# Moving q and k between partition halves with ScalarE and GpSimd in the first batch

## The chip, the cores and the metric

The kernel runs on one core of a Trainium2 chip. A core has a matrix engine (TensorE: PE for the products, PEld for the loads of its weights), VectorE (DVE), ScalarE (ACT) and GpSimd (POOL), each of which works through its own queue of instructions in order, and SyncE (SP), whose queue here issues all DMA transfers; 16 DMA engines carry them out. On-chip memory has 128 partitions. An engine's copy may read from one half of the partitions and write to the other.

The metric is the device time of one execution in microseconds (us).

## The reference

Attention with a cluster mask, followed by a feed-forward network with a maximum over three products:

```python
q_assign = np.argmax(np.einsum('bhsd,hcd->bhsc', q_n, c_n), axis=-1)
k_assign = np.argmax(np.einsum('bhsd,hcd->bhsc', k_n, c_n), axis=-1)
mask = q_assign[:, :, :, None] == k_assign[:, :, None, :]
scores = scale * np.matmul(q, k.transpose(0, 1, 3, 2))
scores = np.where(mask, scores, -1000000000.0)
attn = softmax(scores)            # with 1e-9 added to the sum
x = (attn @ v)                    # [b s, h d]
h = np.maximum(np.maximum(x @ w1, x @ w2), x @ w3)
out = h @ w_out
```

There are 4 batches, 8 heads, 768 positions, 64 dimensions a head and 16 clusters; the network has width 512 and 768 hidden columns. The inputs are float32, the weights float64.

## The kernel before

Products of float32 numbers are made of parts. Each of q and k is split into hi and lo, so that a score is a sum of products of parts. Two heads (a *pair*) are prepared together. The input has q of a head in partitions 0 to 63 and k in partitions 64 to 127, so the preparation of a pair begins with both in the same columns and must bring parts of k to the lower half and parts of q to the upper half. The tile `qk` of a pair has four blocks of two heads by 768 columns, named `AQ, BQ, BK, AK`; in the end they hold [q lo; q hi], [q hi; onehot], [k hi; onehot of k] and [k hi; k lo].

For a pair, in order:

- `qk_prep` (L357), once for each head: SP loads the head (L352), ScalarE copies its hi part into BQ (L362), and VectorE or GpSimd (nearly always GpSimd) subtracts to put the lo part into AQ (L365).
- `cluster_scores` (L397): PE multiplies both parts by the centroids.
- `qk_moves` (L367): three transfers between places on the chip. L370 takes k hi from the upper half of BQ and writes it to the lower halves of BK and AK, 768 KB by the profile's account. L371 copies k lo within the upper half from AQ to AK, 384 KB. L372 takes q hi from the lower half of BQ to the upper half of AQ, 384 KB; since it writes what L371 reads, it waits for L371.
- `cluster_rows` (L415): VectorE and GpSimd find the cluster of each position (L420 to L438). Four small transfers (L448) write the onehot rows into BQ and BK. All pairs use one buffer, `cl_t`, which is free again once these transfers have landed.

The first pair of all has its own moves, by ScalarE (`first_k_moves`) and GpSimd (`first_q_moves`). Two pairs keep their onehot rows in DRAM and load them again later (L390).

The attention goes in steps, `scores` (L470): one step is 128 queries of a head against its 768 keys. PE makes the scores (L475, L477; the second needs the onehot rows), VectorE scales and finds the maximum (L480), ScalarE takes the exponential (L483), then ScalarE and VectorE split the probabilities into two float16 parts (L493, L494), or for some steps GpSimd and ScalarE (L489 to L491). SP issues a transposing transfer (L495), and two steps after the head's last one PE multiplies by v (L505, L508). The first batch goes through its heads twice, with half of the queries each time; pair 0 is loaded and prepared a second time for that. So `qk_moves` is called four times in the first batch: for pairs 1, 2, 3 and again for pair 0. After that it is called for each pair of the three later batches.

During the first batch the float64 weights are loaded (L192), made into float32 by ScalarE and VectorE (L194, L196), and split (L205 to L207). The feed-forward network (L540 to L591) of one half or batch runs beside the attention of the next; that of the last batch stands alone at the end.

The order of each engine's instructions is planned when the program is built. The kernel gives every piece of work a priority, mostly the number of its step plus an offset (the pair after the first has `P1_LATE = -10`, so ten steps early), and a planner with a model of the times (`schedule_with_timeline_sim=True`, L759) picks, for each engine, what is ready and has the best priority. On the chip the order is fixed, and semaphores hold back what isn't ready.

Of the kernel before, what the change touches and what calls it, by code (L numbers as in the profile page):

```python
# [8 lines left out]
F32 = mybir.dt.float32  # L9
# [14 lines left out]
def kernel(  # L24
# [11 lines left out]
    """Cluster-masked softmax attention followed by a three-way maxout FFN.  # L36

    Float32 products are split exactly. Scores and cluster scores use float32r parts
    (x = hi + lo, 12 significant bits each); the probabilities, values and the FFN use
    float16 parts of operands scaled by powers of two that come from the largest  # L40
    magnitude of the operand, found on the chip.

    The argmax over the clusters is the same for q and for q / (|q| + 1e-6), a positive
    factor per row, so only the centroids are normalised. The mask is a product of one-hot
    rows inside the score product: it adds 0 where the clusters agree and -2^100 where
    they don't, which absorbs the score.
    """
# [48 lines left out]
    def pow2_scale(cols, name):  # L96
        """p: the power of two at or below the largest magnitude; s = 2^14 / p; on all partitions."""
        m = sb.tile([P, 1], F32, tag="sc_m", name="sc_m", bufs=2)
        nc.vector.tensor_reduce(m, cols, axis=AX.X, op=ALU.max)
        nc.vector.tensor_scalar_max(m, m, 1e-30)  # L100
        nc.vector.tensor_scalar(m.bitcast(I32), m.bitcast(I32), 0x7F800000, None, op0=ALU.bitwise_and)
        a = one()[:, 0:P]
        nc.tensor.matmul(a, m.bitcast(BF16)[:, 1:2].broadcast_to([P, P]), ident16, start=True, stop=True)
        p = cpool.tile([P, 1], F32, name=f"p_{name}")
        s = cpool.tile([P, 1], F32, name=f"s_{name}")
        nc.vector.tensor_reduce(p, a, axis=AX.X, op=ALU.max)
        nc.vector.reciprocal(s, p)
        nc.vector.tensor_scalar_mul(s, s, 2.0**14)
        return p, s

    # A load that would run too far ahead is held back to the last step of the attention that
    # has been issued: one element of its tile is first written from the sums of that step.
# [56 lines left out]
    # The weights come as float64; the chip makes float32 of their bits, cut after 23 of the  # L169
    # fraction. The doubles land one halfword off, so that the upper three halfwords are  # L170
    # [fraction 16..31 | fraction 0..15] in one aligned word, and [sign, exponent, four bits]
    # in one that reads as bfloat16. Its upper 8 exponent bits of 11, as float16, have the bias
    # that float32 has for all 11: the float16 bits are the upper 13 bits of the result.
    # Each block of 128 hidden columns has its own power of two; the rows of w_out that
    # meet it carry the ratio to the largest.
# [10 lines left out]
    def convert(wp, src, a, d):  # L186
        """src: int16 quarters of float64 in DRAM [P, a, 4m]; d: float32 [P, a * m] on chip."""
# [155 lines left out]
    # Rows of the input: q of a head over k of it. Per pair of heads:  # L343
    # [q lo; q hi], [q hi; onehot], [k hi; (onehot - 1) 2^100], [k hi; k lo].
# [21 lines left out]

    def qk_moves(b, pr):  # L367
        t = qkt[b, pr].bitcast(F32)
        up, dn = slice(0, D), slice(D, 2 * D)
        nc.sync.dma_start(out=t[up, BK : AK + 1], in_=t[dn, BQ : BQ + 1].broadcast_to([D, 2, 2, S]))  # L370
        nc.sync.dma_start(out=t[dn, AK], in_=t[dn, AQ])  # L371
        nc.sync.dma_start(out=t[dn, AQ], in_=t[up, BQ])  # L372

    # The first pair of all doesn't wait for transfers between partitions.
# [93 lines left out]
    # The probabilities are divided by the sums of their rows as they are split (largest 2^14).  # L468
    # Vector has the most to do: Pool splits some of the tiles.
# [128 lines left out]
    # The first batch goes through its heads twice, one half of the queries at a time, so that  # L598
    # the FFN can start on the first half; q and k of three of its pairs stay on chip.
    V_0, W_0 = 4, 9  # L600
    # Vector's part where a task can go to either: 1; Pool's: 0. The last two pairs of QK_LO are
    # the first of the second batch and the first pair when it is loaded again.
# [33 lines left out]
    def spread(units, first, last, late=0):  # L636
        """Put the units at even distances between two steps; the scheduler sees them later by `late`."""
        for i, u in enumerate(units):
            k = first + i * (last - first) / len(units)
            plan.setdefault(max(int(k // 1), 0), []).append((k + late, u))  # L640
# [122 lines left out]
```

## Time and profile before

| | |
|---|---|
| time, median of 3 runs | 869.12 us (867.17 to 874.3) |
| span of the profiled execution, first to last instruction | 866.7 us |
| PE, PEld busy | 719.4 us (83%), 422.7 us (49%) |
| VectorE, ScalarE, GpSimd busy | 611.4 us (71%), 518.0 us (60%), 494.4 us (57%) |
| DMA | 149.86 MB, mean 173 GB/s |

The page gives no time of the profiled execution other than its span; the lowest of the three runs is 0.5 us above it, the median 2.4.

In a row of a timeline stand the start in us, the duration in us, engine, line, operation, the tiles written and read, their shapes, how many instructions are merged, and in brackets the idle time of the engine before it with what ended that. A row such as `SPq L370` is the issue of a transfer, not the transfer; "DMA to landing" counts from the start of the issue to the arrival. In the row of a line stand the shortest, middle and longest duration in ns. A row of the waits gives the total in us, how often, and the longest.

### The profile page before, as it was taken

The page shows a single profiled execution, that of the slowest core. Times are in us where ns is not written, and L with a number is a line of the kernel's source. Part 1 is how long each engine was busy: PE and PEld are TensorE (multiplying, and loading weights), DVE is VectorE, ACT ScalarE, POOL GpSimd, SP SyncE. Part 2 cuts the span into 40 slices and gives each one's busy share as a digit, 9 for nine tenths or more (in the row PEclk, how much of TensorE's full clock was granted, in tenths as well). Part 3 has the DMA queues.
Part 4 walks back from the last instruction along what each step waited for, and adds up shares of the span by engine and source line. Part 5 has one row for each costly group of instructions (what it writes and reads, how often), then busy time and mean ns, then how long its engine had stood idle before and what let it go on. Part 6 is the DMA issues. An engine that isn't in the chain of part 4 may idle for free.

```text
span 866.7 us, 12102 instructions
## 1 busy us (share of the span) xinstructions
PE 719.4 (83%) x3836; PEld 422.7 (49%) x3836; DVE 611.4 (71%) x1327; ACT 518.0 (60%) x907; POOL 494.4 (57%) x486
## 2 busy tenths in 40 slices
PE   3445576767688998989898989989898999999997
PEld 2322343344354565545565545545555565556463
DVE  6777988798989898977798766876587667411020
ACT  6555668754867587868585756765767577510101
POOL 5687783583957374765786555785575446412111
PEclk9656576887889999999999999999999999999999
DMA  8999878999999999999999999897898676810100
GB/s 263 244 200 207 190 156 166 219 227 185 242 184 217 231 196 204 215 176 221 227 198 202 223 211 170 168 228 164 171 175 156 148 148 110 158 43 1 37 1 36
DMA packets 331263, 149.86 MB, mean 173 GB/s; under 512 B 304704, under 2 KB 313920, under 8 KB 331200
## 3 DMA queue, kind: packets, MB, share of 16 engines
q1 hardware_dynamic: 331200, 149.10, 83.2%
q8 instruction: 30, 0.49, 0.2%
q14 instruction: 33, 0.27, 0.1%
HBM read 38.57 MB, written 7.08 MB: 53 GB/s over the span
## 4 chain that ended last, share of the span: by engine, by line
PE 27%; DMA 19%; DVE 14%; ACT 9%; issue 7%; POOL 5%; SPq 2%; ACTq 0%; POOLq 0%; DVEq 0%
DMA pt<-hl 17%; PE one L546 13%; PE one L580 7%; DVE hl L494 5%; DVE big L480 4%; ACT e L483 3%; ACT hl L493 3%; PE one L505 2%; DMA stage<-in_v_dram 2%; POOL hl L491 2%; PE one L508 1%; PE big L475 1%; DVE onehot L434 1%; PE big L477 1%; SPq L495 1%
## 5 line engine op out<-in xcount | busy, mean ns | idle before, releaser
L494 DVE SCALAR_TENSOR_TENSOR hl<-e,r,hl 128x768 f16<-128x768 f32 x147 | 194.3, 1326 | 48.0 <-ACT hl L493 45.2
L546 PE MATMUL one<-x,w16a 128*128 128x384 f16 x1152 | 205.9, 332 | 18.2 <-DVE vf_h L558 9.8
L483 ACT ACTIVATE e<-big,nm 128x768 f32<-128x768 f32 x192 | 172.1, 897 | 77.4 <-DVE big L480 31.4
L480 DVE TENSOR_SCALAR_CACHE_REDUCE big<-big 128x768 f32<-128x768 f32 x192 | 181.8, 959 | 12.7 <-PE big L477 12.2
L493 ACT ACTIVATE hl<-e,r 128x768 f16<-128x768 f32 x147 | 135.9, 931 | 72.7 <-DMA pt<-hl 62.4
L475 PE MATMUL big<-qk 128*128 128x512 f32 (+1 forms) x384 | 128.0, 417 | 61.4 <-ACT e L483 59.6
L546 PEld LDWEIGHTS <-w16a 128*128 128x128 f16 x1152 | 110.2, 99 | 100.8 <-issue 36.1
L477 PE MATMUL big<-qk 80*128 80x512 f32 (+1 forms) x384 | 111.6, 374 | 15.5 <-DMA qk<-cl_t 12.7
L475 PEld LDWEIGHTS big<-qk 128*128 128x128 f32 x384 | 68.2, 209 | 96.0 <-ACT e L483 77.1
L546 PE MATMUL one<-x,w16b 128*128 128x384 f16 x576 | 101.8, 331 | 6.1 <-ACT xt L514 2.6
L505 PE MATMUL one<-pt,v 128*128 128x384 f16 x384 | 84.6, 358 | 17.3 <-DMA pt<-hl 9.1
L491 POOL TENSOR_TENSOR hl<-e,hl 128x768 f16<-128x768 f32 x45 | 77.6, 1730 | 27.6 <-ACT hl L490 27.1
L477 PEld LDWEIGHTS big<-qk 80*128 80x128 f32 x384 | 67.2, 212 | 28.2 <-issue 11.2
L546 PEld LDWEIGHTS <-w16b 128*128 128x128 f16 x576 | 55.1, 99 | 46.7 <-issue 13.7
L365 POOL TENSOR_TENSOR qk<-stage,qk 128x768 fp32r<-128x768 f32 x32 | 64.2, 2021 | 17.9 <-ACT qk L362 17.8
L518 POOL TENSOR_TENSOR xs<-xs,xt 128x384 f32<-128x384 f32 x32 | 34.7, 1084 | 61.9 <-ACT xt L514 61.9
L558 DVE SCALAR_TENSOR_TENSOR vf_h<-one,vf_h 128x384 f32<-128x384 f32 x48 | 26.4, 550 | 51.5 <-PE one L546 51.5
L505 PEld LDWEIGHTS <-v 128*128 128x128 f16 x384 | 37.1, 106 | 50.9 <-issue 24.9
L564 POOL TENSOR_SCALAR wf_h<-wf_h 128x384 f16<-128x384 f32 x24 | 15.5, 647 | 77.0 <-DVE wf_h L558 73.1
L489 POOL TENSOR_SCALAR e<-e,r 128x768 f32<-128x768 f32 x45 | 46.5, 1035 | 21.1 <-DVE r L485 9.6
L558 DVE SCALAR_TENSOR_TENSOR wf_h<-one,wf_h 128x384 f32<-128x384 f32 x48 | 26.5, 551 | 45.4 <-PE one L546 45.2
L490 ACT CAST hl<-e 128x768 f16<-128x768 f32 x45 | 37.2, 830 | 33.6 <-DMA pt<-hl 20.0
(130 smaller groups left out, 1042.8 us busy)
## 6 DMA issues: line engine op xcount, KB each, us to landing
stage<-in_qk_dram SPq DMA_DIRECT2D x36, 384.0 KB, 4.6
qk<-qk SPq DMA_DIRECT2D x16, 768.0 KB, 7.0
qk<-qk SPq DMA_DIRECT2D x32, 384.0 KB, 5.0
stage<-in_v_dram SPq DMA_DIRECT2D x25, 384.0 KB, 4.8
wd<-in_moe_w_dram SPq DMA_DIRECT2D x18, 512.0 KB, 4.6
out_dram<-o SPq DMA_DIRECT2D x24, 256.0 KB, 2.4
pt<-hl SPq DMA_TRANSPOSE x192, 4.3
wd<-in_moe_w_out_dram SPq DMA_DIRECT2D x6, 512.0 KB, 5.9
```

Of the source, the lines that this page charges most:

```text
L365: last["lo"] = eng.tensor_tensor(t[:, AQ, i], x, t[:, BQ, i].bitcast(F32), op=ALU.subtract)
L475: nc.tensor.matmul(t[:, lo:hi], aq[:, qs], ak[:, lo:hi], start=True, stop=False)
L477: last["pe"] = nc.tensor.matmul(t[:, lo:hi], bq[0:K2, qs], bk[0:K2, lo:hi], start=False, stop=True)
L480: last["nm"] = nc.vector.tensor_scalar(e, e, -SCALE, 3.0e38, op0=ALU.mult, op1=ALU.min, accum_out=nm)
L483: nc.scalar.activation(x, e, AF.Exp, bias=nm, scale=-1.0, accum_out=r)
L491: nc.gpsimd.tensor_tensor(hl[:, 1, :], x, hl[:, 0, :], op=ALU.subtract)
L493: nc.scalar.activation(hl[:, 0, :], x, AF.Copy, scale=r)
L494: nc.vector.scalar_tensor_tensor(hl[:, 1, :], x, r, hl[:, 0, :], op0=ALU.mult, op1=ALU.subtract)
L505: nc.tensor.matmul(t[:, 0:NB], vt, pt[:, :, kt, :], start=(kt == 0), stop=False)
L546: nc.tensor.matmul(t[:, 0:NB], w16[jt // JA][:, jt % JA, wa, i, ct], x16[b, gi, ct][:, xa, :], start=(n == 0), stop=(n == 3 * CT - 1),)
L558: nc.vector.scalar_tensor_tensor(m, t[:, 0:NB], 2.0**-24, ms[jt], op0=ALU.mult, op1=ALU.max)
L580: nc.tensor.matmul(t[:, 0:DM], h16[jt][:, ha, tt * P : (tt + 1) * P], wo16[0][:, jt, wa, :], start=(n == 0), stop=(n == 3 * JT - 1),)
```

## The change

In the first batch alone, the move of k hi and the move of q hi are made by engines. The transfer of k lo (L371) stays. In the later batches nothing changes.

```diff
     def qk_moves(b, pr):
-        t = qkt[b, pr].bitcast(F32)
+        t = qkt[b, pr]
+        x = t.bitcast(F32)
         up, dn = slice(0, D), slice(D, 2 * D)
-        nc.sync.dma_start(out=t[up, BK : AK + 1], in_=t[dn, BQ : BQ + 1].broadcast_to([D, 2, 2, S]))
-        nc.sync.dma_start(out=t[dn, AK], in_=t[dn, AQ])
-        nc.sync.dma_start(out=t[dn, AQ], in_=t[up, BQ])
+        if b:
+            nc.sync.dma_start(out=x[up, BK : AK + 1], in_=x[dn, BQ : BQ + 1].broadcast_to([D, 2, 2, S]))
+        else:
+            nc.scalar.copy(t[up, AK], x[dn, BQ])
+            nc.scalar.copy(t[up, BK], x[dn, BQ])
+        nc.sync.dma_start(out=x[dn, AK], in_=x[dn, AQ])
+        if b:
+            nc.sync.dma_start(out=x[dn, AQ], in_=x[up, BQ])
+        else:
+            nc.gpsimd.tensor_scalar(t[dn, AQ], x[up, BQ], 1.0, 1.0, op0=ALU.mult, op1=ALU.mult)
```

Each of the two ScalarE copies and the GpSimd copy writes 64 partitions by 1536 columns. Beside this the diff only takes out comments, with the numbers of the lines kept up to the changed function.

## The prediction

> **What bounds the kernel now.** I read the page first, for the span and the engines, then the busy time by stretches, because an average over the span mixes stages.
>
> ```profile
> span 866.7 us, 12102 instructions
> ...
> wd<-in_moe_w_dram SPq DMA_DIRECT2D x18, 512.0 KB, 4.6
> ...
> qk<-cl_t SPq DMA_DIRECT2D x56, 48.0 KB, 2.2
> ```
>
> ```profile
> 0.00:50.00 50.00, 20.25 (x54) 13.26 (x54) 39.03 (x74) 30.23 (x51) 32.15 (x48) 0.80 0.94 248
> 50.00:100.00 50.00, 31.57 (x104) 17.87 (x104) 39.03 (x83) 28.21 (x50) 37.71 (x38) 0.59 0.94 202
> 400.00:600.00 200.00, 180.12 (x1034) 108.48 (x1033) 153.51 (x340) 138.38 (x246) 133.53 (x118) 0.99 0.98 200
> ```
>
> The columns of the last three are stretch, length, busy time of PE, PEld, DVE, ACT and POOL, granted clock, DMA share and GB/s. Between 400 and 600 us PE is busy for 90% of the time: it is the bound there. In the first 100 us it is not: PE works 20.25 and 31.57 us of 50, VectorE 39 of 50, while the DMA engines are at 0.94. The three early calls of the changed function lie there, and the fourth at 157 us. So I asked whether somebody waits for a DMA in those places, and then followed the chain of waits and the timelines of single engines around them.
>
> ```profile
> 38.28 0.77 ACT L194 CAST top<-wd 128x512 f16<-128x512 bf16 x1 [5.47 <-DMA wd<-in_moe_w_dram]
> 39.08 0.69 DVE L196 SCALAR_TENSOR_TENSOR wf<-wd,top 128x512 int32<-128x512 int32 x1 [3.86 <-ACT top L194]
> L192 SPq DMA_DIRECT2D wd<-in_moe_w_dram x2: 541/1197/1853, 28.7 to 31.5; - x2
> DMA to landing us min/median/max: 9.6/10.2/10.8
> 49.61 2.92 SPq L448 DMA_DIRECT2D qk<-cl_t  x4
> DMA to landing us min/median/max: 4.6/5.0/5.7
> 56.36 1.62 PE L477 MATMUL big<-qk 80*128 80x512 f32 x4 [5.07 <-DMA qk<-cl_t]
> ```
>
> The first landing line is that of the two weight loads above it, the second that of the four L448 rows. This is one chain. ScalarE stands at the head of its queue for a weight load that took 9.6 us, twice the kernel's median of 4.6. VectorE idles 3.86 us behind it, with the onehot rows of pair 1 (heads 2 and 3) queued behind that; the rows go out at 49.61, need about 5 us where 2.2 is usual, and PE starts pair 1 at 56.36. It is a queue of transfers, and the moves of q and k are in it:
>
> ```profile
> 17.01 0.74 SPq L370 DMA_DIRECT2D qk<-qk  x1
> 21.31 1.80 SPq L370 DMA_DIRECT2D qk<-qk  x1
> 27.61 0.97 SPq L372 DMA_DIRECT2D qk<-qk  x1
> 41.05 0.51 SPq L372 DMA_DIRECT2D qk<-qk  x1
> 42.30 1.82 SPq L370 DMA_DIRECT2D qk<-qk  x1
> 157.77 0.70 SPq L370 DMA_DIRECT2D qk<-qk  x1
> 158.57 17.53 DMA pt<-hl x2
> SPq L372 <- DMA qk<-qk: 5.4, 2, 3.6
> 176.12 0.93 ACT L493 ACTIVATE hl<-e,r 128x768 f16<-128x768 f32 x1 [5.33 <-DMA pt<-hl]
> ```
>
> The 17.53 us are a piece of the chain that ended last: two transposes, issued right behind the 768 KB move at 157.77, and ScalarE waits 5.33 us for them.
>
> **The change, part by part.** *Removed*, four times (pairs 1, 2, 3, and pair 0 when it is loaded again): a 768 KB and a 384 KB transfer, 4.72 MB. At the first stretch's rate (248 GB/s at 0.94 busy, 264 GB/s when full) that is 3.0 + 1.5 = 4.5 us of the DMA engines a pair, 17.9 us in all. This is the most that the transfers can give; the least is nothing. I take what a wait shows:
> - Ahead of the weight load of 28.7 us stand two large moves and one small, 7.5 us; the first has landed by then, but it counts where the queue behind it has not run empty. Even without it, 4.5 us, most of ScalarE's 5.47 goes. The 7.5 is more than ScalarE's 5.47, so VectorE's 3.86 us go whole: -3.9.
> - Ahead of the rows of 49.61 stand the small move of 41.05 and the large one of 42.30, 4.5 us. The rows could come nearer to 2.2 by 2.8 us; the transposes ahead of them stay, so I take -2.0 (0 to -2.8).
> - At 157.77 the transposes lose 3.0 us of queue: -3.0, 0 to -5.3. SP's wait at L372, 3.6 us, also goes from SP; next late there is the load of v, which stands behind the same move and comes earlier with it.
>
> Together -8.9. SP's issue times (0.5 to 1.8 us each) go as well; I count them at nothing, since SP stood behind the same queue.
>
> *Added*, on ScalarE: two copies of 64x1536 a pair.
>
> ```profile
> L379 ACT CAST qk<-stage x2: 831/831/831, 6.8 to 9.3; 64x768 fp32r<-64x768 f32 x2
> 16.15 2.75 ACT L362 CAST qk<-stage 128x768 fp32r<-128x768 f32 x3 [1.58 <-DMA stage<-in_qk_dram]
> 22.75 0.90 ACT L483 ACTIVATE e<-big,nm 128x768 f32<-128x768 f32 x1 [3.85 <-DVE big L480]
> 25.49 0.77 ACT L194 CAST top<-wd 128x512 f16<-128x512 bf16 x1 [1.75 <-DVE wf L196]
> ```
>
> Twice 0.83 is 1.66 us a copy, 3.3 us a pair, 13.3 in all. They need only the casts of L362, on the same engine, and space that nobody reads, so ScalarE doesn't wait for another engine. Pairs 1 and 2 are cast by 18.90; 6.6 us of copies meet idle stretches of 3.85 and 1.75: 1.0 over. For pair 3 I take the same share, 0.5. The fourth stands ahead of the idle 5.33 us above, of which the relief of 3.0 leaves 2.3: 1.0 over. Together +2.5, and 13.3 if all that cover is gone.
>
> *Added*, on GpSimd: one copy a pair, with a new wait. It overwrites q's low rows, which the remaining transfer (L371) must have read. SP used to wait for this; now GpSimd does, and all of its queue waits behind.
>
> ```profile
> L386 POOL TENSOR_SCALAR qk<-qk x2: 827/827/827, 9.7 to 11.8; 64x768 fp32r<-64x768 f32 x2
> 27.31 1.49 POOL L426 TENSOR_TENSOR cl_t<-cl_t 128x384 f32<-128x384 f32 x1 [2.40 <-DVE r L484]
> 174.81 0.91 POOL L334 TENSOR_SCALAR stage<-stage,s_v 128x768 f32<-128x768 f32 x1 [4.09 <-DMA stage<-in_v_dram]
> ```
>
> A copy of 64x1536 is 1.65 us, 6.6 in all. For pair 1 GpSimd has 2.40 us free before the onehot sum at 27.31; for the fourth, 4.09 before 174.81. I take +0.7 for a wait that overruns the first gap. The bound upwards is a rival below.
>
> GpSimd also slows VectorE when both run:
>
> ```profile
> L494 DVE SCALAR_TENSOR_TENSOR hl<-e,r,hl x51: 976/1136/5728, 30.7 to 299.7; 128x768 f16<-128x768 f32 x51
> L494 DVE SCALAR_TENSOR_TENSOR hl<-e,r,hl 128x768 f16<-128x768 f32 x51 | 73.8, 1455 | 4.3 <-ACT hl L493 3.8
> 16.35 0.56 DVE L434 TENSOR_TENSOR onehot<-rank,cl_m 128x384 f32<-128x384 f32 x1
> 188.91 7.39 DVE L434 TENSOR_TENSOR onehot<-rank,cl_m 128x384 f32<-128x384 f32 x1
> ```
>
> In 300 us the 51 splits of L494 took on average 1455 - 976 ns over their shortest, 24.4 us together. GpSimd is busy for 32.15 + 37.71 of the first 100 us, so for about 200 of 300: 0.12 us for one. 6.6 us more of GpSimd add 0.8. The other end is a VectorE that stands still for all of it, 6.6. I take 0.8: it comes from 51 instructions, the 7.39 from one.
>
> The Trainium skill, SBUF — State Buffer, "Who interferes with whom", has a rule here: VectorE instructions with two SBUF inputs and GpSimd instructions that read SBUF share a port pair as an exclusive lock, and the later one blocks fully. The trace agrees: the same instruction takes 0.56 us or 7.39. What the sum would be by the rule stands with the rivals.
>
> Sum: -8.9 + 2.5 + 0.7 + 0.8 = -4.9. The profiled execution's 866.7 become 861.8. The median of the runs, 869.12, lies 2.4 above that span: **864.2 us**. All later work is ordered behind the first batch, and PE bounds most of it, so I let the shift through to the end whole.
>
> **The rivals.**
> *The queue itself sets the pace.* For: the share of 0.94 in both early stretches. Then all 17.9 us show: -17.9 + 4.0 = -13.9, 855.2. Against: VectorE is at 78%, and much of the relief lies where it is busy.
>
> *GpSimd stalls (slower).* L371 stays in SP's queue, behind transposes, and lands late:
>
> ```profile
> L371 SPq DMA_DIRECT2D qk<-qk x1: 1556/1556/1556, 29.3 to 29.3; - x1
> DMA to landing us min/median/max: 10.8/10.8/10.8
> L371 SPq DMA_DIRECT2D qk<-qk x1: 537/537/537, 52.6 to 52.6; - x1
> DMA to landing us min/median/max: 5.4/5.4/5.4
> 41.53 3.59 POOL L365 TENSOR_TENSOR qk<-stage,qk 128x768 fp32r<-128x768 f32 x2 [2.71 <-ACT qk L362]
> ```
>
> These are pairs 2 and 3. If the order puts pair 2's copy ahead of L426 at 27.31, GpSimd waits until 40.1 less the 7.5 us of relief, 32.6: 5.3 + 1.7 = 7.0 late, and the rows of pair 1 with it. If pair 3's stands right behind L365, which ends at 45.1, it waits until 58.0 less 3.0: 9.9 + 1.7 = 11.6. Both are 18.6, less the forecast's 4.9: +13.7, 882.8. Pair 3's alone gives 875.8. It decides from the point where a copy stands ahead of softmax or onehot work in GpSimd's queue. For: the order comes from a cost model that need not know this queue. Against: that model also delays the copy by the transfer that it expects.
>
> *The lock takes it.* By that mechanism at its full price, VectorE stands still for 6.6 us instead of 0.8: +0.9, 870.0. It is the skill's rule named above; the mean of L494 speaks against it.
>
> *The relief is hidden.* If VectorE's order, and no landing, sets the time of the rows, nothing is gained and 4.0 paid: 873.1.
>
> **How the numbers follow.** Chances: forecast 0.44 (its own range 857 to 870: the relief at 157.77 may be 5.3, ScalarE's copies may be covered or not, and the planned order may change elsewhere), queue 0.22, stalls 0.17, lock 0.07, hidden 0.10. One per cent, about what a measurement of this kernel can tell from no change, is 860.4 to 877.8. Faster: the queue case and a little over a third of the forecast's, 0.38. Slower: most of the stalls, and a few of the hidden and the lock's, 0.18. Within: 0.44. The range from 850 to 877 leaves out the far half of the stalls and the ends of the others.
>
> **What would show it.** Right: no ScalarE wait of 5 us for wd near 38 us; the rows of pair 1 out by about 46 and pair 1 on PE by about 50.5; ScalarE's wait at 176 down to about 2; VectorE's L494 mean in 300 us near 1.47. Wrong: a GpSimd wait for qk<-qk of over 5 us with L426, L489 or L491 right behind it, an L434 or L494 of many microseconds beside a GpSimd copy, or a start of pair 1 that doesn't move.

## The result and the profile after

The changed kernel takes **879.87 us** (median of 5, 876.03 to 884.62), the kernel before 869.12. The ratio is 1.0107, with a 95% interval from 1.0076 to 1.0138: about 1% slower. (The quotient of the two medians is 1.012, inside that interval.) The forecast was 864.2 us, and its range ended at 877.

In the changed file every line behind the edited function stands 9 lower: L480 has become L489, L494 L503, L448 L457. The GpSimd copy is L381, the ScalarE copies are L375 and L376, the transfer of k lo is L377. The profile is that of the slowest of the five executions (884.62 us), so the spans of the two profiles differ by 16.1 us where the medians differ by 10.75. First the page of the changed kernel, and its busy time by stretches (stretch, length, PE, PEld, DVE, ACT, POOL, granted clock, DMA share, GB/s; a share counts a packet whole in the stretch in which it starts, so it can pass 1):

```profile
span 882.8 us, 12105 instructions
...
q1 hardware_dynamic: 330304, 144.38, 79.1%
```

```profile
0.00:50.00 50.00, 18.96 (x53) 12.33 (x53) 42.78 (x84) 37.75 (x55) 32.34 (x48) 0.83 0.81 234
50.00:100.00 50.00, 25.71 (x87) 15.47 (x87) 37.05 (x60) 23.53 (x43) 38.21 (x39) 0.59 0.60 124
250.00:300.00 50.00, 36.87 (x179) 21.30 (x178) 47.17 (x118) 31.53 (x55) 22.79 (x23) 0.83 0.84 176
300.00:350.00 50.00, 43.74 (x232) 25.55 (x231) 31.32 (x69) 29.89 (x52) 24.48 (x23) 0.90 0.90 182
```

The same for the kernel before, where the prediction doesn't show it:

```profile
250.00:300.00 50.00, 41.97 (x221) 24.01 (x220) 47.34 (x110) 33.94 (x59) 25.08 (x24) 0.93 1.04 219
300.00:350.00 50.00, 46.00 (x273) 28.32 (x272) 44.60 (x97) 35.81 (x63) 33.19 (x32) 1.00 1.04 206
```

The transfers are gone (149.10 MB in that queue before, 144.38 now), and the DMA share of the first 100 us falls from 0.94 to 0.81 and 0.60. Yet PE does less in the same time (25.71 us instead of 31.57 between 50 and 100), and in the last two stretches, whose code the change doesn't touch, it does less again.

To see where the time goes I number the steps of the attention by their score reductions (L480 before, L489 after), from 0; each starts once in the profile. The first batch ends near step 48, the second near 96.

| start of step, us | 6 | 36 | 39 | 60 | 78 | 96 | 138 | 186 |
|---|---|---|---|---|---|---|---|---|
| before | 57.6 | 159.0 | 181.3 | 285.4 | 343.9 | 400.4 | 550.7 | 724.2 |
| after | 66.9 | 162.8 | 177.0 | 283.3 | 358.0 | 409.5 | 566.7 | 740.4 |
| after less before | +9.3 | +3.8 | -4.4 | -2.2 | +14.1 | +9.1 | +16.0 | +16.2 |

So the profiles show two losses, neither of which begins at a moved operation: 9 us before step 6, won back by step 39, and 18 us from step 60 to step 138. A single difference of a few us is not to be trusted: two of the runs below (e5, e9) have every queue in the order of the changed kernel until past step 60, and their step 60 starts at 277.4 and 281.2 us, not at 283.3. Timelines of the changed kernel at both places, in order of time:

```profile
50.34 3.25 SPq L457 DMA_DIRECT2D qk<-cl_t  x4
56.79 1.62 PE L486 MATMUL big<-qk 80*128 80x512 f32 x4 [0.97 <-DMA qk<-cl_t]
57.80 8.62 DVE L503 SCALAR_TENSOR_TENSOR hl<-e,r,hl 128x768 f16<-128x768 f32 x1
57.95 1.78 POOL L339 TENSOR_TENSOR v<-vf,v 128x384 f16<-128x384 f32 x2
59.70 1.62 POOL L500 TENSOR_TENSOR hl<-e,hl 128x768 f16<-128x768 f32 x1
61.29 0.99 POOL L435 TENSOR_TENSOR cl_t<-cl_t 128x384 f32<-128x384 f32 x1
62.25 3.36 POOL L207 TENSOR_TENSOR w16a<-wf,w16a 128x512 f16<-128x512 f32 x3
66.95 0.95 DVE L489 TENSOR_SCALAR_CACHE_REDUCE big<-big 128x768 f32<-128x768 f32 x1
69.04 0.79 PE L412 MATMUL big<-qk,cw 128*128 128x512 f32 x1 [9.35 <-ACT e L492]
71.55 0.41 PE L413 MATMUL big<-qk,cw 128*128 128x256 f32 x1
72.12 1.47 POOL L381 TENSOR_SCALAR qk<-qk 64x1536 fp32r<-64x1536 f32 x1 [6.52 <-DVE r L494]
176.69 0.92 ACT L338 CAST v<-stage 128x384 f16<-128x384 f32 x2 [1.47 <-POOL stage L334]
305.76 2.67 SPq L457 DMA_DIRECT2D qk<-cl_t  x4
310.63 4.53 SPq L292 DMA_DIRECT2D stage<-in_v_dram  x2
313.84 0.95 DVE L293 TENSOR_REDUCE vmax<-stage 128x1 f32<-128x768 f32 x1 [1.22 <-DMA stage<-in_v_dram]
315.73 5.30 SPq L504 DMA_TRANSPOSE pt<-hl  x2
318.46 0.95 DVE L293 TENSOR_REDUCE vmax<-stage 128x1 f32<-128x768 f32 x1 [3.41 <-DMA stage<-in_v_dram]
319.33 0.96 DVE L489 TENSOR_SCALAR_CACHE_REDUCE big<-big 128x768 f32<-128x768 f32 x1
```

Near 58 us VectorE stands in L503 for 8.62 us beside GpSimd instructions without a gap, and steps 6 to 8 stand behind it. The delay then reaches the change's own copy for pair 3 (72.12), ahead of which GpSimd idles 6.52 us with softmax work queued behind. The row names VectorE's `r`, which the copy doesn't read. But the copy overwrites rows that the centroid products (L413) read, and it starts 0.16 us after the last of them has ended (71.96); these products are late because PE stands 9.35 us for an exponential (69.04), and ScalarE makes that from the scores held up behind L503.

Near 313 us VectorE's queue holds two maxima of v (L293) ahead of step 67. Each needs a load into a staging buffer, and the second load goes out only when the first maximum has freed its buffer, behind which the transposes of 315.73 stand in SP's queue too. In the kernel before, the same place reads:

```profile
304.06 5.17 SPq L495 DMA_TRANSPOSE pt<-hl  x3
309.32 2.72 SPq L448 DMA_DIRECT2D qk<-cl_t  x4
311.54 0.95 DVE L480 TENSOR_SCALAR_CACHE_REDUCE big<-big 128x768 f32<-128x768 f32 x1
316.19 0.93 DVE L293 TENSOR_REDUCE vmax<-stage 128x1 f32<-128x768 f32 x1
322.86 0.94 DVE L293 TENSOR_REDUCE vmax<-stage 128x1 f32<-128x768 f32 x1
```

Step 67 (311.54) stands ahead of both maxima, and three transposes ahead of the rows. Nothing in the diff asks for that difference: the planner has made a new order of every queue, from start to end, because a few operations of the first batch differ.

### The profile page after: what moved, and what is told of

It reads as the page before. It is cut to its first block, busy times and chain, and to the rows that moved or that the text cites. A ratio compares the mean times of both kernels' runs of the same rounds, so it can differ in the third digit from the quotient of the medians.

```text
span 882.8 us, 12105 instructions
## 1 busy us (share of the span) xinstructions
PE 722.7 (82%) x3836; PEld 425.1 (48%) x3836; DVE 617.5 (70%) x1327; ACT 529.3 (60%) x915; POOL 498.3 (56%) x490
## 3 DMA queue, kind: packets, MB, share of 16 engines
q1 hardware_dynamic: 330304, 144.38, 79.1%
## 4 chain that ended last, share of the span: by engine, by line
PE 26%; DMA 15%; DVE 13%; ACT 7%; issue 6%; POOL 4%; SPq 2%; ACTq 0%; POOLq 0%; DVEq 0%
PE one L555 13%; DMA pt<-hl 12%; PE one L589 6%; DVE big L489 4%; DVE hl L503 4%; ACT hl L502 3%; DMA stage<-in_v_dram 2%; PE one L514 2%; ACT e L492 2%; SPq L504 1%; POOL hl L500 1%; PE big L484 1%; PE one L517 1%; PE big L486 1%; DVE cl_t L441 1%
## 5 line engine op out<-in xcount | busy, mean ns | idle before, releaser
L503 DVE SCALAR_TENSOR_TENSOR hl<-e,r,hl 128x768 f16<-128x768 f32 x147 | 194.9, 1331 | 56.7 <-ACT hl L502 54.6
L489 DVE TENSOR_SCALAR_CACHE_REDUCE big<-big 128x768 f32<-128x768 f32 x192 | 181.6, 960 | 16.2 <-PE big L486 15.7
L514 PE MATMUL one<-pt,v 128*128 128x384 f16 x384 | 82.5, 356 | 38.0 <-DMA pt<-hl 15.3
L500 POOL TENSOR_TENSOR hl<-e,hl 128x768 f16<-128x768 f32 x45 | 78.9, 1759 | 45.4 <-ACT hl L499 44.9
L498 POOL TENSOR_SCALAR e<-e,r 128x768 f32<-128x768 f32 x45 | 43.7, 975 | 28.0 <-DVE r L494 21.0
```

The source lines that it names most:

```text
L489: last["nm"] = nc.vector.tensor_scalar(e, e, -SCALE, 3.0e38, op0=ALU.mult, op1=ALU.min, accum_out=nm)
L500: nc.gpsimd.tensor_tensor(hl[:, 1, :], x, hl[:, 0, :], op=ALU.subtract)
L503: nc.vector.scalar_tensor_tensor(hl[:, 1, :], x, r, hl[:, 0, :], op0=ALU.mult, op1=ALU.subtract)
L514: nc.tensor.matmul(t[:, 0:NB], vt, pt[:, :, kt, :], start=(kt == 0), stop=False)
```

## Experiments

**How an order is laid on a program.** In the kernels e1 to e11, e14 and e15 the program is built twice for its plan and once more to run. `FROM` names the moves with which the program is planned whose order is wanted, `RUN` those of the program that runs (for the first four calls of `qk_moves`: "k" by ScalarE, "q" by GpSimd, both, or neither). Neighbours in a queue are tied by edges that cost no semaphore:

```python
for q in order.values():
    made = [by[k] for k in q]
    for a, b in zip(made, made[1:]):
        tc.add_manual_dep(b, a.name, mybir.DependencyInfo(mybir.DependencyClass.NoSync, mybir.DependencyReason.DATA), reason="pin")
```

`PLACE` is the instruction ahead of which a copy stands, `MOVE` takes one instruction to ahead of another in its queue, and `CUT` changes from one order to another at a step; their numbers count the program's instructions. The diffs below give these settings in short form. The profiles show what came of it: VectorE's 1327 instructions start in the same order in e1 as in the kernel before, and in e2 as in the changed kernel. In these files the GpSimd copy is L382, the ScalarE copies L376 and L377, the transfer of k lo L378; the other lines are those of the changed kernel.

### The change in the order of before, and the reverse

```diff
 # e1
+FROM, RUN = {}, {0: "kq", 1: "kq", 2: "kq", 3: "kq"}
 # e2
+FROM, RUN = {0: "kq", 1: "kq", 2: "kq", 3: "kq"}, {}
```

> The change with the order of every engine's queue as in the kernel before: edges without a semaphore put each instruction behind its neighbour of before, and the new copies stand where the changed kernel has them, beside the same neighbours. Theory (the planner made a new order of all queues from start to end, and that order costs the time; the moved operations themselves gain a little): ratio to the kernel before 0.985 to 1.000, so some 856 to 869 us, and the stretch from 285 to 345 us costs no more than before. Rival 1 (the operations cost it: ScalarE and GpSimd time, the wait of a GpSimd copy, the port): ratio 1.007 to 1.02, so 875 to 886 us.

> The other half of the pair: the transfers between the halves as in the kernel before, with the order of every queue as in the changed kernel. Theory (the order costs): ratio to the kernel before 1.007 to 1.025, so 875 to 891 us, with the loss again in the second batch, between 285 and 345 us. Rival 1 (the operations cost): 0.995 to 1.003, so 865 to 872 us.

| | time, us | ratio to before, 95% |
|---|---|---|
| e1: the change, order of before | 866.34 | 0.9968 [0.995, 0.9986] |
| changed kernel: the change, its own order | 879.87 | 1.0107 [1.0076, 1.0138] |
| e2: the transfers, order of the changed kernel | 888.74 | 1.0225 [1.019, 1.026] |

This settles the main question. The operations gain in either order: 0.3% in that of before, and 1.0225 against 1.0107, so 1.2%, in the new one. The order costs 1.4% with the copies and 2.25% with the transfers. The loss of the change is the loss of the order, less the gain of the operations. The kernel before with its own order laid on it wasn't run, so a cost of the edges themselves isn't known; if they cost something, the operations gain more than e1 shows, and the order costs more.

### One half of the change at a time

```diff
 # e3
+FROM, RUN = {}, {0: "k", 1: "k", 2: "k", 3: "k"}
 # e4
+FROM, RUN = {}, {0: "q", 1: "q", 2: "q", 3: "q"}
```

> The order of before, with the high part of k alone moved by ScalarE and q left to its transfer. Theory: 512 KB leave the queue ahead of pair 1's rows, against two ScalarE copies of about 1.47 us for each pair; ratio 0.988 to 1.001. Rival 1 (the operations cost, here ScalarE's): 1.003 to 1.01. If the GpSimd copies are what costs, this run gains and the one with q alone loses.

> The order of before, with q alone moved by GpSimd and k left to its transfer. Theory: 256 KB leave the queue and GpSimd gets 1.5 to 1.8 us for each pair; ratio 0.992 to 1.002. Rival 2 (the lock: a GpSimd copy makes a back-to-back run of GpSimd instructions in which VectorE stands, as at 57.8 us of the changed kernel, 8.62 us): 1.006 to 1.015, with one VectorE instruction of over 5 us beside the copy.

(By the profile's account the transfers are of 768 and 384 KB, not of 512 and 256.) k alone gave 0.9968 [0.9939, 0.9997], q alone **1.0102** [1.0064, 1.0139]: the theory fell for q. The timelines of e4:

```profile
38.23 1.47 POOL L382 TENSOR_SCALAR qk<-qk 64x1536 fp32r<-64x1536 f32 x1 [7.38 <-DMA qk<-qk]
39.78 0.84 POOL L440 TENSOR_TENSOR cl_t<-cl_t,cl_m 128x384 f32<-128x384 f32 x1
59.22 1.62 PE L486 MATMUL big<-qk 80*128 80x512 f32 x4 [1.76 <-DMA qk<-cl_t]
62.46 5.51 DVE L503 SCALAR_TENSOR_TENSOR hl<-e,r,hl 128x768 f16<-128x768 f32 x1
```

GpSimd waits 7.38 us for the transfer of pair 2's k lo. Behind it stands L440 for pair 1, and PE gets pair 1's rows at 59.22, where the kernel before had them at 56.36. This is the stall of the prediction's second rival. Step 6 starts at 60.7, 4.6 us later than in e1, and then step 8 stands behind an L503 of 5.51 us, which puts it 8.4 us behind e1 (67.9 against 59.5). So the rival of e4's expectation is there too, though the GpSimd run in which L503 stands (L205, L500, L435) ends just ahead of the copy. In e1 (the first of the next two), where k's large transfers are gone, k lo lands sooner; e3 (the second) has no GpSimd copy:

```profile
33.17 1.98 POOL L382 TENSOR_SCALAR qk<-qk 64x1536 fp32r<-64x1536 f32 x1 [1.66 <-DMA qk<-qk]
35.24 0.84 POOL L440 TENSOR_TENSOR cl_t<-cl_t,cl_m 128x384 f32<-128x384 f32 x1
51.14 2.47 SPq L457 DMA_DIRECT2D qk<-cl_t  x4
54.59 1.65 PE L486 MATMUL big<-qk 80*128 80x512 f32 x4 [1.67 <-DMA qk<-cl_t]
```

```profile
30.92 0.84 POOL L440 TENSOR_TENSOR cl_t<-cl_t,cl_m 128x384 f32<-128x384 f32 x1 [0.39 <-DVE cl_m L436]
47.77 2.48 SPq L457 DMA_DIRECT2D qk<-cl_t  x4
51.30 1.62 PE L486 MATMUL big<-qk 80*128 80x512 f32 x4 [1.72 <-DMA qk<-cl_t]
```

To test the stall, e15 leaves q alone with GpSimd and moves one transfer: the 768 KB of k of pair 2 go behind pair 2's k lo.

```diff
 # e15
 FROM, RUN = {}, {0: "q", 1: "q", 2: "q", 3: "q"}
+MOVE = {"EngineType.SP": [((1, "k0"), 683)]}
```

> The run with q alone, but with the 512 KB transfer of k of pair 2 behind the transfer of pair 2's low part of k. In the run with q alone the GpSimd copy of pair 2 waited 7.38 us for that landing, with L440 and L500 behind it. Theory (GpSimd's wait is what made q alone 1.010): the wait falls to 1 to 3 us; ratio 0.998 to 1.004. Rival (the port, VectorE beside the GpSimd copies): still 1.007 to 1.012.

```profile
36.55 1.47 POOL L382 TENSOR_SCALAR qk<-qk 64x1536 fp32r<-64x1536 f32 x1 [5.85 <-DMA qk<-qk]
38.10 0.84 POOL L440 TENSOR_TENSOR cl_t<-cl_t,cl_m 128x384 f32<-128x384 f32 x1
57.53 1.62 PE L486 MATMUL big<-qk 80*128 80x512 f32 x4 [1.73 <-DMA qk<-cl_t]
```

The wait fell less than expected (7.38 to 5.85), and the ratio went from 1.0102 to 1.0049 [1.0022, 1.0076], just outside the theory's range and with an interval that still overlaps e4's. Of the 5.1 us by which step 9 comes sooner than in e4 (71.0 against 76.1), 1.7 are the stall's and the rest the L503's: with all this 1.7 us earlier, VectorE gets its turn, and no L503 there takes over 3 us. That the copy sits in pair 1's chain is shown by four runs: L440 starts at 30.92, 35.24, 38.10, 39.78 and PE takes pair 1 at 51.30, 54.59, 57.53, 59.22, so 19.4 to 20.4 us later each time. So q alone has both mechanisms, the stall and a blocked VectorE behind it; their shares of the 1.0% hang on where the two engines happen to meet.

### Where the new order loses

With the change in all of them (`ALL` is the `RUN` of e1), the order goes over at step 60 (twelve steps into the second batch) or 90:

```diff
 # e6: changed kernel's order to step 60, then that of before
+FROM, RUN, CUT, TAIL = {}, ALL, 1767, False
 # e7: order of before to step 60, then the changed kernel's
+FROM, RUN, CUT, TAIL = {}, ALL, 1796, True
 # e14: the same, over at step 90
+FROM, RUN, CUT, TAIL = {}, ALL, 2666, True
```

> The change, with the first batch (until step 60 of the scores) in the order of the changed kernel and all that follows in the order of before. Theory (the loss of the changed kernel comes from the order in the second batch): 0.994 to 1.002, as the profile of the changed kernel stands 2 us ahead at step 60. Rival (the order of the first batch leaves something behind, in buffers or loads, that the second pays for): 1.006 to 1.012.

> The change, with the first batch in the order of before and all that follows in the order of the changed kernel. Theory (the order in the second batch costs): 1.006 to 1.016. Rival (the first batch's order leaves something behind that costs): 0.994 to 1.000.

> The change, with the order of before until step 90 of the scores, and that of the changed kernel behind it. In the profiles of the runs with the changed kernel's order behind step 60, steps 60 to 75 lose 9 to 16 us, some 5 are won back by step 84, and steps 96 to 138 lose 8 more. If these are two separate places: ratio 1.002 to 1.007 (the second alone). If the loss of 96 to 138 is only what the first left over: 0.995 to 1.000.

Measured were 1.0033 [1.0008, 1.0058], 1.0082 [1.0057, 1.0107] and 1.0029 [1.0009, 1.005]. So the order of steps 60 to 90 costs 0.5% (e7 against e14) and that behind 90 0.6% (e14 against e1's 0.9968). The profiles bear these two out: steps 60 to 138 take 265 to 272 us in the five that keep the order of before (the kernel before, e1, e3, e4, e15), and 279 to 284 us in four with the changed kernel's (the changed kernel, e2, e7, e8).

e6 came out 0.65% above e1, and above the range that the theory gave it. That is not the price of the first batch's order alone, for e6 loses time where its two orders meet: step 60 follows step 59 by 16.2 us (16.3 in e11, below, with the same change of order), against 9.2 to 10.1 in the kernel before and in every other run e1 to e10. In the profiles e6 is 4.7 us behind e1 at step 59, 11.2 at step 60, and 4.5 again at step 138. Together the three come to 1.8%, where the whole order has 1.4%. So the loss lies in at least two stretches, both behind step 60; what the first batch's order costs by itself is open.

Could single places be named? e5 moves the three transposes ahead of the rows, as before; e9 also moves the two maxima with their loads, from ahead of step 67 to just ahead of steps 70 and 73 (in the kernel before they stand ahead of 69 and 72); e8 moves the L503 of 57.80 behind two score reductions; e10 is e8 and e9 together. All of them run the change.

```diff
 # e5
+MOVE = {"EngineType.SP": [(1890, 2045), (1914, 2045), (1942, 2045)]}
 # e9
+MOVE = {"EngineType.DVE": [(2436, 2128), (2501, 2164), (2615, 2142), (2616, 2188), (2617, 2188)],
+        "EngineType.SP": [(1890, 2045), (1914, 2045), (1942, 2045), (2500, (7, "k0")), (2622, (7, "k0"))]}
 # e8; e10 has this and that of e9
+MOVE = {"EngineType.DVE": [(277, 340)]}
```

> The changed kernel in its own order, but for three transposes of the sync engine's queue: in the changed kernel they stand behind the rows of a pair, two loads of v and a result (idle of that queue between 299.26 and 315.73 us); here they stand ahead of the rows, as in the kernel before. Theory (the second batch loses its 10 us at this one place, where loads that wait for a buffer stand ahead of transposes that are ready): ratio to the kernel before from 1.011 down to 0.997 to 1.004, and step 72 of the scores no later than 2 us against before. Rival (the loss is spread over many changed places in all queues): 1.007 to 1.012.

> The changed kernel in its own order, but for one VectorE instruction: L503 that took 8.62 us at 57.80, beside a run of GpSimd instructions without a gap, stands behind two score reductions instead of ahead of them. Theory (it is the kind of instruction that stands still beside GpSimd, and the two reductions do not): steps 6 and 7 of the scores start 6 to 9 us sooner (58 to 61 us), L503 still waits for the end of the GpSimd run; the time goes down by 0 to 5 us, as the delay of 9 us at step 6 was made up by step 39 anyway: ratio 1.004 to 1.011. Rival 2 (the lock at this place is what costs the 10 us): 0.996 to 1.002. If the reductions stand still in its place: no change at step 6.

> The changed kernel in its own order, but for one place in the second batch: the two maxima of v (VectorE, L293) and the three small instructions behind them stand behind the score reductions 67 to 70 again, as in the kernel before, and the loads that feed them (L292) and the three transposes stand in the sync engine's queue with the transposes first. Theory (VectorE's queue is blocked there: the second maximum waits for a load that waits for the buffer of the first, 12.50 us in the run with the transposes alone moved, 3.41 us in the changed kernel, and the scores stand behind it): step 67 of the scores follows step 66 within 3 us instead of 8; ratio to the kernel before 0.999 to 1.006, against 1.011. Rival (loss spread over many places): 1.007 to 1.013.

> The run with the maxima as before, and L503 behind two score reductions at 58 us too. Theory (two places of the new order make nearly all of the loss): ratio 0.993 to 1.001, as the change in the order of before has 0.997. Rival: 1.003 to 1.010.

| | ratio, 95% | step 6 | 60 | 66 | 67 | 70 | 78 |
|---|---|---|---|---|---|---|---|
| before | 1 | 57.6 | 285.4 | 308.7 | 311.5 | 318.7 | 343.9 |
| after | 1.0107 [1.0076, 1.0138] | 66.9 | 283.3 | 311.1 | 319.3 | 326.8 | 358.0 |
| e5 | 1.0198 [1.0143, 1.0252] | 67.0 | 277.4 | 302.5 | 322.2 | 326.8 | 355.5 |
| e9 | 1.0146 [1.0102, 1.019] | 67.0 | 281.2 | 306.9 | 310.3 | 322.4 | 355.2 |
| e8 | 1.0062 [1.0032, 1.0092] | 58.6 | 273.7 | 299.6 | 308.0 | 316.1 | 345.9 |
| e10 | 1.0118 [1.0052, 1.0185] | 59.4 | 272.0 | 299.1 | 302.7 | 314.6 | 345.8 |

e5 missed: a wait was handed on and grew. With the transposes first, the loads of v go out later, and VectorE, which has the maxima ahead of step 67, stands longer (timeline of e5):

```profile
316.56 0.95 DVE L293 TENSOR_REDUCE vmax<-stage 128x1 f32<-128x768 f32 x1 [12.50 <-DMA stage<-in_v_dram]
321.37 0.95 DVE L293 TENSOR_REDUCE vmax<-stage 128x1 f32<-128x768 f32 x1 [3.60 <-DMA stage<-in_v_dram]
```

e9 did what it was meant to do for step 67 (3.4 us after step 66 instead of 8.2) and still lost: step 70 now comes 10 us behind step 69, with the first maximum now just ahead of it (timeline of e9):

```profile
321.43 0.95 DVE L293 TENSOR_REDUCE vmax<-stage 128x1 f32<-128x768 f32 x1 [2.56 <-DMA stage<-in_v_dram]
322.36 0.95 DVE L489 TENSOR_SCALAR_CACHE_REDUCE big<-big 128x768 f32<-128x768 f32 x1
```

With this order steps 60 to 78 take 74 to 78 us in the changed kernel, e5, e9 and e10, 72.2 in e8 and 67.6 in e7, against 58.4 before, whatever is done at one place. e8 put step 6 back at 58.6. Its profile is 12 us ahead of the changed kernel's to the end, its ratio 0.45% lower, 4 us, with intervals that overlap. Two more pairs of runs differ in this one move alone: e10 lies 0.28% below e9, and e11 (next) 0.25% below e6. Each pair's intervals overlap, but all three go the same way, so one VectorE instruction at 58 us may hold 2 to 4 us of the loss, and it is the only place to which the runs give a price at all. The moves of e9 didn't help e10: it lies above e8.

One more run took e8's head, with the largest lead of any at step 48, and put the order of before behind it:

```diff
 # e11
+FROM, RUN, CUT, TAIL = {}, ALL, 1767, False
+MOVE = {"EngineType.DVE": [(277, 340)]}
```

> The change, with the first batch (until step 60) in the order of the changed kernel but L503 behind two score reductions, and all that follows in the order of before. If the 11.7 us that the run with L503 moved was ahead at step 60 are kept in the order of before: ratio 0.985 to 0.993. Rival (the lead is lost again behind step 60, as the second batch waits for something that doesn't come sooner): 0.996 to 1.003.

It gave 1.0008 [0.998, 1.0037], which is the rival. The lead over the kernel before, 11.7 us at step 48 of the profile and 11.4 at step 59, is 4.8 at step 60, where the order goes over. So most of it went at the meeting of the two orders, as in e6, and not behind step 60, where the rival had it.

### Other plans of the same operations

Is the order of the changed kernel bad because of the change? These runs leave the operations of either kernel alone and change one offset of the planner by half a step.

```diff
-    PREP, PREP_END, PREP_LATE = 2, 5, -9
+    PREP, PREP_END, PREP_LATE = 2, 5, -9.5
```

(e12 of the kernel before, e13 of the changed one; e18 has -8.5, of the kernel before.)

```diff
-    W_LATE, F_LATE, AV_LATE = -5, 0, 2
+    W_LATE, F_LATE, AV_LATE = -5, 0.5, 2
```

(e17 of the kernel before, e16 of the changed one.)

> The kernel before, its operations untouched, planned anew: the offset of the preparation of pairs is -9.5 steps instead of -9. Theory (a new plan alone moves the time by as much as this change did): the ratio lies off 1 by 0.005 to 0.02, more likely above 1 than below. Rival (plans are worth the same within what can be measured, and the order of the changed kernel is bad for a reason of the change): 0.997 to 1.003.

> The changed kernel, its operations untouched, planned anew with the offset of the preparation of pairs at -9.5 steps instead of -9. Theory (the time of the changed kernel is that of one of many plans, and the operations are worth a little less than nothing): the ratio to the kernel before moves by 0.004 or more from 1.0107, to somewhere from 0.994 to 1.018, more likely down. Rival (the operations bring a bad plan whatever the offset): 1.008 to 1.014.

> The changed kernel, its operations untouched, planned anew with the offset of the feed-forward network at 0.5 step instead of 0. Theory (one of many plans): the ratio moves by 0.004 or more from 1.0107, to somewhere from 0.994 to 1.018. Rival (the operations bring a bad plan whatever the offset): 1.008 to 1.014.

> The kernel before, its operations untouched, planned anew with the offset of the feed-forward network at 0.5 step instead of 0, as in the run of the changed kernel with that offset (1.0087). Theory (the order of before is one of the better among its like, and any new plan loses some): ratio 1.003 to 1.015. Rival (plans with the transfers as before are worth the same, and those with the copies are worse): 0.997 to 1.003.

> The kernel before, its operations untouched, planned anew with the offset of the preparation of pairs at -8.5 steps instead of -9 (with -9.5 it was 1.0048). Theory (any new plan loses some): ratio 1.003 to 1.015. Rival (plans with the transfers are worth the same): 0.997 to 1.003.

| offset | transfers | copies (the change) |
|---|---|---|
| as it is | 1 | 1.0107 [1.0076, 1.0138] |
| preparation -9.5 | 1.0048 [1.0025, 1.0071] | 1.0201 [1.0168, 1.0235] |
| network 0.5 | 1.0123 [1.0062, 1.0184] | 1.0087 [1.0054, 1.012] |
| preparation -8.5 | 1.0085 [1.005, 1.012] | not tried |

Half a step of an offset moves the time of the kernel before by 0.5 to 1.2% and that of the changed one by 0.9% (e13) or by nothing that can be told (e16), with the operations unchanged: about as much as the change did. e12 came out just under the range of its theory, e13 went the other way than was thought likely and out of its range, e16 stayed where the rival had it, and e17 and e18 lie in their ranges. All three new plans of the kernel before are slower than the one it has. With the network's offset at 0.5 the two columns are the same within their intervals. So the order of before is a good one among its like, and the change lost it. Whether plans with the copies are on average worse than plans with the transfers isn't settled by three against three.

## Why the prediction was wrong

**The step that failed** is the sum itself: it prices operations and waits one by one in the order of before, and has no term for a new order. The text had it only as an aside in the forecast's own range ("the planned order may change elsewhere", 857 to 870), and then let "the shift through to the end whole". The order is worth +1.4%, +12 us; the operations, in the order that the sum assumed, are worth -0.3%, -2.8 us (forecast: -4.9). No rival had this mechanism.

The second half of the step, "the shift through to the end whole", fails even in the order of before. e1's profile is 5.9 us ahead of the kernel before at step 60, about what the sum forecast, 3.2 at step 96 and 0.4 at step 138, and its runs gain 2.8 us at the end (its profile is of the slowest of them). Part of what the first batch gains is lost again later; which later wait takes it is open.

Point by point:

- *The weight load (-3.9).* Right in the order of before: between 20 and 60 us ScalarE never waits for a weight load in e1 (at L194 its longest wait is 1.3 us, for VectorE). In the changed kernel ScalarE's waits there are (who, for whom, total, times, longest):

```profile
ACT top L194 <- DMA wd<-in_moe_w_dram: 6.7, 3, 3.2
```

  That is no 5 us wait near 38, but three shorter ones at other places, which a new order has made.
- *Rows of pair 1 (-2.0; rows out by 46, PE by 50.5).* Together with the first point pair 1 should have come 5.9 us sooner. k alone, in the order of before: PE at 51.30, 5.1 sooner. With GpSimd's copy, e1: 54.59, 1.8 sooner. In the changed kernel the start did not move (56.79), which the text had listed as a sign that it was wrong: there VectorE did other planned work first, the rows went out at 50.34, and they took 3.9 to 5.9 us to land, behind a weight load of 49.90. In the order of before they land in 2.1 us in e1 and e3, near the 2.2 that the text hoped for, though they go out at 51.14 and 47.77.
- *Transposes at 157.77 (-3.0, up to -5.3).* Right, near the upper end. ScalarE's wait of 5.33 at 176 is gone (1.47, for GpSimd, is left there), and from step 36 to 39 the profiles need 17.3 us (e1) and 16.0 (e3) where ScalarE moves k hi, and 22.3 (the kernel before, e15) and 23.5 (e4) where a transfer does, all in the order of before.
- *ScalarE's copies (1.66 us each, +2.5).* They take 1.47. k alone, which has them and no GpSimd copy, is 5.1 us ahead at pair 1, which leaves them 0.8 there, if the relief was the 5.9 of the forecast; no run separates the two.
- *GpSimd's copy and wait (+0.7).* Mis-sized. The copy stands ahead of the onehot work (L440), as the stall rival had it: between e3 and e1 it costs 3.3 us at pair 1. The rival's price, 18.6 us, needed landings as late as before; with k's transfers gone k lo lands sooner and GpSimd waits 1.66 us. Leave k's transfers in place, and the stall comes: 7.38 us and 1.010 in q alone. The text also left out a second thing that the copy waits for, the centroid products that read the rows it overwrites. In the changed kernel this is the longer wait: 6.52 us ahead of pair 3's copy, with softmax work (L498) right behind, where the longest wait for the landing is 1.62. In e8, where the scores come sooner, it is gone. No run gives it a price of its own.
- *VectorE beside GpSimd (+0.8).* The mean of the splits in 300 us should have been near 1.47 us. The changed kernel and e1, by groups of their first 300 us:

```profile
L503 DVE SCALAR_TENSOR_TENSOR hl<-e,r,hl 128x768 f16<-128x768 f32 x50 | 73.4, 1472 | 8.5 <-ACT hl L502 8.4
```

```profile
L503 DVE SCALAR_TENSOR_TENSOR hl<-e,r,hl 128x768 f16<-128x768 f32 x51 | 77.5, 1526 | 5.8 <-ACT hl L502 5.5
```

  In the changed kernel (the first row) the mean is as forecast, and it hides what matters: 8.62 us in one instruction, at a place where the new order had put three score reductions behind it. In the order of before, which the sum assumed, it isn't: 1526 ns in e1 is 3.6 us more over 51 splits than 1455, where the text took 0.8, and e3, without the GpSimd copies, has 1382. *The lock* as a rival (every GpSimd copy paid in full) is not what made the change slow: the blocking run of 57.95 to 65.61 holds no copy of the change, and e1 gains with its longer splits.
- *The queue sets the pace* (855.2) was wrong: the DMA share fell to 0.60 and the time did not follow. *GpSimd stalls* (875.8 to 882.8) has the measured 879.87 in between, by luck: the landing that it counts on held GpSimd for 1.62 us at most.

In ratios: +1.07% is -0.32% for the operations in the old order and +1.39% for the order. Shown is that the order costs it, and that steps 60 to 90 and those behind 90 each hold a part; which changed places there make it, and what the order of the first batch adds, is open.

## What to carry to other kernels

Where a planner orders the queues, a change of a few operations is also a new order of all of them. Measure the two apart: lay the old order on the new program, and plan the old program anew with a harmless offset to see what an order is worth (here 0.5 to 1.2%, against 0.3% for the operations). A change that gains in the old order and loses in the planned one is worth keeping with the old order: e1, 0.9968, beats both kernels here.

Before work goes to an engine that has to wait for a landing, look at what stands behind it in that engine's queue; the price is the landing's lateness, and that falls if the same change takes other transfers out of the way.

## What the runs showed of the hardware

- VectorE can be kept from its turn over several GpSimd instructions that follow each other without a gap. The long L503 and L494 end 0.81 to 0.82 us after the end of the GpSimd run: 66.42 behind 65.61 in the changed kernel, and 130.20 behind 129.38 in the kernel before (timelines):

```profile
124.47 5.73 DVE L494 SCALAR_TENSOR_TENSOR hl<-e,r,hl 128x768 f16<-128x768 f32 x1
128.48 0.90 POOL L520 TENSOR_TENSOR x<-xs,x 128x384 f16<-128x384 f32 x1
```

  In e8 it is the same with six L339 in a row (the same instruction, with every queue in the same order up to there, took 1.25 us in the changed kernel, so it hangs on how the two engines happen to meet):

```profile
48.46 6.60 DVE L503 SCALAR_TENSOR_TENSOR hl<-e,r,hl 128x768 f16<-128x768 f32 x1
53.34 0.90 POOL L339 TENSOR_TENSOR v<-vf,v 128x384 f16<-128x384 f32 x1
58.61 0.96 DVE L489 TENSOR_SCALAR_CACHE_REDUCE big<-big 128x768 f32<-128x768 f32 x1
60.40 1.48 DVE L503 SCALAR_TENSOR_TENSOR hl<-e,r,hl 128x768 f16<-128x768 f32 x1
61.02 1.72 POOL L435 TENSOR_TENSOR cl_t<-cl_t 128x384 f32<-128x384 f32 x1
```

  The price of sharing can then be the length of the run without a gap, and not that of one GpSimd instruction. The score reductions, with one input, ran at their 0.96 us beside the same work (58.61). The last two lines go against the expectation for e8: the moved L503 did not wait for the end of the run, it got in, and GpSimd's L435 took 1.72 us instead of 0.99. Who gets in between two instructions isn't explained by these runs. The Trainium skill (SBUF — State Buffer, "Who interferes with whom") has the later of the two block fully; the traces agree, and show that it can last over several instructions.
- Between 250 and 350 us the stretches in which PE waits more also have the lower granted clock: 0.83 with PE busy 36.87 of 50 us, 0.93 with 41.97 (250 to 300 us, changed kernel and before), 0.90 with 43.74 and 1.00 with 46.00 (300 to 350). It is no rule: the changed kernel's first 50 us have 0.83 with 18.96, the next 50 only 0.59 with 25.71. Whether a wait ahead of PE is paid a second time in the clock isn't separated by any run here.
